# Turning similarities and one-hots on VectorE in 32 by 32 blocks instead of on TensorE, with a reordered first head pair

## The chip, the cores and the metric

One core of a Trainium2 chip. A core has a matrix engine (TensorE, PE in the profile; its weight loads are listed apart as PEld), a vector engine (VectorE, DVE), a scalar engine (ScalarE, ACT), a general engine (GpSimd, POOL) and DMA queues, which run beside each other and wait for each other by semaphores. Matrix products land in PSUM; the other data is in SBUF, both with 128 partitions. The metric is the device time of one execution in microseconds (us), the median of several.

## What is computed

Routing attention, followed by a mixture of experts. Each query and each key of a head goes to the nearest of 16 centroids, and a query sees only the keys with the same centroid. The result is the input of eight experts, of which each row uses one.

```python
# q, k, v: (4, 8, 768, 64) f32; centroids: (8, 16, 64)
q_assign = np.argmax(np.einsum('bhsd,hcd->bhsc', q_n, c_n), axis=-1)   # q_n, k_n, c_n: normalised
k_assign = np.argmax(np.einsum('bhsd,hcd->bhsc', k_n, c_n), axis=-1)
mask = q_assign[:, :, :, None] == k_assign[:, :, None, :]
scores = scale * np.matmul(q, k.transpose(0, 1, 3, 2))                 # scale = 1/8
scores = np.where(mask, scores, -1000000000.0)
attn = softmax(scores)                                                 # written out in the reference
x = np.matmul(attn, v)                                                 # -> (3072, 512) rows
# experts: logits = x @ w_gate; e = argmax; y = relu(x @ w1[e]) @ w2[e], times the gate
```

## The kernel before

The kernel handles two heads at a time, a "pair"; there are 16 pairs g = 0..15, four to a batch. The 768 queries of a pair are taken in two halves of 384 (HS), and the keys in six blocks of 128: 12 score units a pair, six (NB) to a "turn" of the schedule, so two turns a pair. P = 128, S = 768, NQ = 6, D = 64, C = 16, G = 24.

For each pair, rows of q and k are transposed by PE into `qk` (64 numbers of two heads on 128 partitions, tokens along the columns). PE then takes the similarities with the centroids; a second set of transposes brings the tokens back onto the partitions; the largest one is found along the columns and made a one-hot; and a third set of transposes puts the one-hots back, centroids on partitions, where they enter the score products as extra rows that make a score hugely negative if the centroids differ.

```python
def turn(g, piece):                       # transposes of q and k rows, copies to qk
    ...
    n = 4 if piece else 8
    for i in range(n):
        w, j = divmod(8 * piece + i, NQ)
        nc.tensor.transpose(ps[:, i * P : (i + 1) * P], rows[g, "qk"[w]][:, j]..., ident)
    if piece == 0:
        if g == 1: nc.scalar.mul(flat[:, 0:S], ps[:, 0:S], D**-0.5)
        else:      nc.vector.tensor_scalar_mul(flat[:, 0:S], ps[:, 0:S], D**-0.5)
        nc.scalar.copy(flat[:, S:1024], ps[:, S:1024])
    else:
        nc.scalar.copy(flat[:, 1024 : 2 * S], ps[:, 0 : 2 * S - 1024])

def similar(g):                           # 4 products into four groups of 32 partitions
    ...
    nc.vector.tensor_copy(sims[g], ps[:, 0:HS])

def similar2(g):                          # tokens onto partitions
    ...
    for i in range(NQ // 2):
        nc.tensor.transpose(ps[:, i * P : (i + 1) * P], simT[:, i * P : (i + 1) * P], ident)
    nc.scalar.copy(sims[g], ps[:, 0:HS]...)

def assign(g):
    nc.vector.tensor_reduce(mx, sim, axis=AX, op=ALU.max)
    nc.vector.tensor_tensor(sim, sim, mx..., op=ALU.is_ge)
    nc.gpsimd.tensor_tensor(sim, sim, first_c..., op=ALU.mult)    # the first of equals

def assign2(g):
    nc.vector.tensor_reduce(top, rank, axis=AX, op=ALU.max)
    for w in range(2):
        nc.vector.tensor_tensor(ohs..., rank..., top..., op=ALU.is_equal)

def put(g):                               # centroids onto partitions again
    ps = wide()[:, 0, :].bitcast(BF16)
    for j in range(NQ):
        nc.tensor.transpose(ps[:, j * P : (j + 1) * P], ohs..., ident_b)
    nc.scalar.copy(oh[:, 0, :], ps[:, 0:S])
    for a in range(2):
        nc.vector.tensor_scalar(oh[a * D : a * D + C, 1, :], ps[...], scalar1=BIG, scalar2=-BIG, op0=ALU.mult, op1=ALU.add)

def score(u):                             # one unit: 2 products with qk, 2 with ohT, then exp
    ps = ps_s.tile([P, 2, 512], F32, name="sps")
    ...                                   # lhsT=qk[g][r, 1, ks], rhs=qk[g][r, 0, qs]
    ...                                   # lhsT=ohT[g][r, 1, ks], rhs=ohT[g][r, 0, qs]
    nc.scalar.activation(A[u], ps[:, :, 0:HS], AF.Exp)
    ...                                   # DVE: T += A[u], the row sums
```

`wide()` takes one of three PSUM buffers named `sps`, in rotation. Every engine works its instructions off in program order. In each turn n the order is: the six scores, the jobs of part 0, the six products with v (`attend`), the jobs of part 1:

```python
at(n - 3, 0, turn, g, 0); at(n - 3, 0, turn, g, 1)      # n = 2 g, for g of 2 and more
at(n - 3, 1, similar, g)
at(n - 2, 0, similar2, g)
at(n - 2, 0, assign, g); at(n - 2, 0, assign2, g)
at(n - 1, 0, put, g)
at(n, 1, finish, g, 0); at(n + 1, 1, finish, g, 1)
at(n + 2, 0, weigh, g); at(n + 2, 1, weigh2, g)         # logits of the experts
at(n + 2, 1, x_turn, g, 0); at(n + 3, 1, x_turn, g, 1)
# at the end of a batch: at(n + 3, 0, gate, ...), at(n + 3, 1, keep_rows, ...)
```

So in odd turns part 0 holds `put` of the next pair and `turn` of the one after it.

Of the kernel before, what the change touches and what calls it, by code (L numbers as in the profile page):

```python
# [185 lines left out]
def kernel(  # L186
# [77 lines left out]
    ps_m = late.enter_context(tc.tile_pool(name="ps_m", bufs=1, space=PSUM))  # L264

    pools = dict(s=ps_s)


    def wide():
        return pools["s"].tile([P, 2, 512], F32, name="sps")  # L270
# [394 lines left out]
    with ExitStack() as actx:  # L665
# [17 lines left out]
        def load_qk(g):  # L683
            b, hp = divmod(g, HP)
            for name, src in (("q", q), ("k", k)):
                t = rows[g, name] = ld.tile([P, NQ, 2, D], F32, name=name + "_in")
                for a in range(2):
                    nc.sync.dma_start(out=t[:, :, a, :], in_=src[b, 2 * hp + a].rearrange("(p j) d -> p j d", j=NQ))

        def load_v(g):  # L690
            b, hp = divmod(g, HP)
# [5 lines left out]

        csb = consts.tile([P, D], F32)
        nc.scalar.dma_start(out=csb, in_=centroids.rearrange("h c d -> (h c) d"))
        wg_in = consts.tile([P, DB, E], F32)  # L700
        nc.scalar.dma_start(out=wg_in, in_=moe_w_gate.rearrange("(a p) e -> p a e", p=P))
        for f in (load_qk, load_v):
            for g in range(2):
                f(g)
        make_identity(nc, ident)
        nc.vector.tensor_copy(ident_b, ident)

        ps = ps_m.tile([P, 512], F32, name="mps")
        for i in range(12):
            nc.tensor.matmul(ps[:, 0:P], lhsT=ident, rhs=ident, start=True, stop=True)  # L710
        first_c = iota("first_c", [P, C], [[-1, C]], C, 0)
        first_e = iota("first_e", [P, E], [[-1, E]], E, 0)

# [2 lines left out]
        one_row = consts.tile([P, 32], F32)  # L716
        nc.gpsimd.memset(one_row, 0.0)
        nc.gpsimd.memset(one_row[:, E : E + 1], 1.0)
        for a in range(2):
            r = slice(a * D, (a + 1) * D)  # L720
            nc.gpsimd.tensor_copy(wg[r, :, a, 0:E], wg_in[r])

        ohs = ohp.tile([P, NQ, 2, 2, 32], BF16, name="oh")
        nc.gpsimd.memset(ohs, 0.0)
        ohTs = []
        for i in range(2):
            t = ohp.tile([P, 2, S], BF16, name=f"ohT{i}")
            nc.gpsimd.memset(t[:, 1, :], 0.0)
            ohTs.append(t)


        csq = consts.tile([P, D], F32)
        cs2 = consts.tile([P, 1], F32)
        nc.scalar.activation(csq, csb, AF.Square, accum_out=cs2)
        cnrm = consts.tile([P, 1], F32)
        nc.scalar.activation(cnrm, cs2, AF.Sqrt)

# [9 lines left out]
        cn = consts.tile([P, 2, D], F32)  # L747
        for a in range(2):
            nc.vector.tensor_scalar(cn[:, a, :], csb, scalar1=cinv[:, 0:1], scalar2=None, op0=ALU.mult)
        cps = ps_m.tile([P, 512], F32, name="mps")  # L750
        nc.tensor.transpose(cps[:, 0:P], cn.rearrange("p a d -> p (a d)"), ident)

        cblk = consts.tile([P, HP, 2, C], F32)
        nc.gpsimd.memset(cblk, 0.0)
        cview = cps[:, 0:P].rearrange("p (g a c) -> p g a c", a=2, c=C)
        for a in range(2):
            nc.vector.tensor_copy(cblk[a * D : (a + 1) * D, :, a, :], cview[a * D : (a + 1) * D, :, a, :])


        qk, sims, ohT = {}, {}, {}  # L760
# [1 line left out]
        def turn(g, piece):  # L762

            if piece == 0:
                qk[g] = qkp.tile([P, 2, S], F32, name="qk")
            ps = ps_s.tile([P, 2, 512], F32, name="sps").rearrange("p a c -> p (a c)")
            n = 4 if piece else 8
            for i in range(n):
                w, j = divmod(8 * piece + i, NQ)
                nc.tensor.transpose(ps[:, i * P : (i + 1) * P], rows[g, "qk"[w]][:, j].rearrange("p a d -> p (a d)"), ident)  # L770
            flat = qk[g].rearrange("p w s -> p (w s)")
            if piece == 0:

                if g == 1:
                    nc.scalar.mul(flat[:, 0:S], ps[:, 0:S], D**-0.5)
                else:
                    nc.vector.tensor_scalar_mul(flat[:, 0:S], ps[:, 0:S], D**-0.5)
                nc.scalar.copy(flat[:, S:1024], ps[:, S:1024])
            else:
                nc.scalar.copy(flat[:, 1024 : 2 * S], ps[:, 0 : 2 * S - 1024])  # L780

        def similar(g):

            ps = wide()[:, 0, :]
            for t in range(4):
                w, half = divmod(t, 2)
                nc.tensor.matmul(  # L787
                    ps[t * 2 * C : (t + 1) * 2 * C, 0:HS], lhsT=cblk[:, g % HP].rearrange("p a c -> p (a c)"),
                    rhs=qk[g][:, w, half * HS : (half + 1) * HS], start=True, stop=True,
                )  # L790
            sims[g] = asg.tile([P, HS], F32, name="simT", bufs=1)
            nc.vector.tensor_copy(sims[g], ps[:, 0:HS])

        def similar2(g):
            simT = sims.pop(g)
            ps = wide()[:, 0, :]
            for i in range(NQ // 2):
                nc.tensor.transpose(ps[:, i * P : (i + 1) * P], simT[:, i * P : (i + 1) * P], ident)
            sims[g] = asg.tile([P, G, C], F32, name="sim")
            nc.scalar.copy(sims[g], ps[:, 0:HS].rearrange("p (t c) -> p t c", c=C))  # L800

        def assign(g):

            sim = sims.pop(g)
            mx = asg.tile([P, G], F32, name="mx")
            nc.vector.tensor_reduce(mx, sim, axis=AX, op=ALU.max)
            nc.vector.tensor_tensor(sim, sim, mx.unsqueeze(2).to_broadcast([P, G, C]), op=ALU.is_ge)  # L807
            nc.gpsimd.tensor_tensor(sim, sim, first_c[:, None, :].to_broadcast([P, G, C]), op=ALU.mult)  # L808
            sims[g] = sim

        def assign2(g):
            rank = sims.pop(g)
            top = asg.tile([P, G], F32, name="top")
            nc.vector.tensor_reduce(top, rank, axis=AX, op=ALU.max)

            v = lambda t, w: t.rearrange("p (i w x) c -> p i w x c", w=2, x=4)[:, :, w]
            for w in range(2):
                nc.vector.tensor_tensor(
                    ohs.rearrange("p (i h) a w c -> p i (h a) w c", h=2)[:, :, :, w, 0:C], v(rank, w),
                    top.rearrange("p (i w x) -> p i w x", w=2, x=4)[:, :, w].unsqueeze(3).to_broadcast([P, NQ // 2, 4, C]),  # L820
                    op=ALU.is_equal,
                )

        def put(g):
            oh = ohT[g] = ohTs[g % 2]
            ps = wide()[:, 0, :].bitcast(BF16)
            for j in range(NQ):
                nc.tensor.transpose(
                    ps[:, j * P : (j + 1) * P],
                    ohs[:, (j % (NQ // 2)) * 2 + j // (NQ // 2)].rearrange("p a w c -> p (a w c)"), ident_b,  # L830
                )

            nc.scalar.copy(oh[:, 0, :], ps[:, 0:S])
            for a in range(2):
                nc.vector.tensor_scalar(
                    oh[a * D : a * D + C, 1, :], ps[a * D + 32 : a * D + 32 + C, 0:S],
                    scalar1=BIG, scalar2=-BIG, op0=ALU.mult, op1=ALU.add,
                )


        A, T, O = {}, {}, {}
# [6 lines left out]
        def score(u):  # L848
# [8 lines left out]
                r = slice(a * D, (a + 1) * D)  # L857
                nc.tensor.matmul(ps[:, a, 0:HS], lhsT=ohT[g][r, 1, ks], rhs=ohT[g][r, 0, qs], start=False, stop=True)  # L858
            A[u] = ap.tile([P, 2, HS], F32, name="A")
            nc.scalar.activation(A[u], ps[:, :, 0:HS], AF.Exp)  # L860
            if j == 1:
                T[g, half] = tp_.tile([P, 2, HS], F32, name="T", bufs=3)
                nc.vector.scalar_tensor_tensor(  # L863
# [109 lines left out]
        def at(n, part, f, *a):  # L973
            jobs.setdefault((n, part), []).append((f, a))
# [7 lines left out]
        for g in range(NG):  # L982
            n = g * TG
            if g == 0:
                at(-4, 0, turn, g, 0)
                at(-4, 1, turn, g, 1)
                at(-3, 0, similar, g)
                at(-3, 1, similar2, g)
            elif g == 1:

                at(-2, 1, turn, g, 0)
                at(-2, 1, turn, g, 1)
                at(-1, 1, similar, g)
                at(0, 0, similar2, g)
            else:
                at(n - 3, 0, turn, g, 0)
                at(n - 3, 0, turn, g, 1)
                at(n - 3, 1, similar, g)
                at(n - 2, 0, similar2, g)
            at(n - 2, 0, assign, g)  # L1000
            at(n - 2, 0, assign2, g)
            at(n - 1, 0, put, g)
            at(n, 1, finish, g, 0)
            at(n + 1, 1, finish, g, 1)
            if g < NG - 1:
                at(n + 2, 0, weigh, g)
# [313 lines left out]
```

## Time and profile before

| | |
|---|---|
| time, median of 3 | 777.03 us (776.28 to 777.63) |
| span of the profiled execution | 776.7 us |
| the attention part | until about 400 us; the experts after it |
| L787, similarities (DVE copy L792 after it) | 128 products of 384 columns; copies 0.56 us |
| L798, transposes of the similarities | 48 of 128x128 f32 |
| L828, transposes of the one-hots | 96 of 128x128 bf16 |
| L867 and L863, row sums on DVE | 0.96 us each, five a turn |
| L835, DVE part of `put` | 0.55 us each, two a pair |

The page of the profile has the busy time of each engine over the span, then the span in 40 slices with the busy tenths of each. The order of time lists the start and length of each group of instructions, the engine, the line of the kernel, and what is written from what; in square brackets it gives the idle time of the engine ahead of it and what ended that. A table by stretches gives, for each stretch of time, the busy time of each engine with its instructions in parentheses, and the clock granted to PE as a share of its full speed.

### The profile page before, as it was taken

What the parts mean: (1) busy time and instruction counts of PE and PEld (TensorE: products, weight loads), DVE (VectorE), ACT (ScalarE), POOL (GpSimd) and SP (SyncE); (2) the same over time, 40 slices, a digit from 0 to 9 for tenths busy, and PEclk for the clock granted to TensorE, in tenths of its full rate; (3) what the DMA queues carried; (4) which work ended last, traced back from release to release, by engine and by line L of the source; (5) the groups of instructions that cost most, each with busy time, mean ns of one, the idle gap of its engine ahead of it and who ended that gap; (6) DMA issues with size and microseconds to landing.
All of it is one profiled execution on the core that took longest, in us unless ns stands there. A gap on an engine that the chain in (4) does not pass through costs nothing.

```text
span 776.7 us, 12417 instructions
## 1 busy us (share of the span) xinstructions
PE 755.2 (97%) x5021; PEld 485.7 (63%) x5021; DVE 449.8 (58%) x758; ACT 299.0 (38%) x481; POOL 111.0 (14%) x157
## 2 busy tenths in 40 slices
PE   6999999999999999999999999999999999999994
PEld 4544555445554455544556668787888898787861
DVE  3667677666676666778743544555564655555200
ACT  4545645556455564555531112232222214132210
POOL 2200000100000000001200541311312121211101
PEclk9999999999999999999999999999999999999998
DMA  9025501455115221120103446747556675847540
GB/s 221 6 62 204 136 26 37 144 208 131 30 33 144 62 62 31 32 103 1 45 1 135 152 127 224 267 166 253 221 216 219 246 261 178 308 155 246 212 156 18
DMA packets 85281, 106.41 MB, mean 137 GB/s; under 512 B 52831, under 2 KB 56927, under 8 KB 84704
## 3 DMA queue, kind: packets, MB, share of 16 engines
q1 hardware_dynamic: 79616, 85.99, 34.9%
q0 software_dynamic: 4928, 19.51, 6.8%
q8 instruction: 41, 0.67, 0.4%
q14 instruction: 24, 0.20, 0.1%
q10 hardware_dynamic: 672, 0.05, 0.1%
HBM read 92.90 MB, written 13.16 MB: 137 GB/s over the span
## 4 chain that ended last, share of the span: by engine, by line
PE 80%; issue 9%; DVE 6%; POOL 2%; ACT 2%; ACTq 0%; POOLq 0%; DVEq 0%
PE sps L855 15%; PE O L875 13%; PE sps L476 10%; PE sps L310 9%; PE sps L498 8%; PE sps L364 7%; PE sps L858 4%; PE mps L896 3%; DVE T L867 3%; PE sps L787 2%; PE sps L344 2%; PE sps L770 2%; PE sps L291 2%; PE sps L941 1%; PE mps L909 1%
## 5 line engine op out<-in xcount | busy, mean ns | idle before, releaser
L860 ACT ACTIVATE A<-sps 128x768 f32<-128x768 f32 x192 | 153.3, 812 | 53.4 <-PE sps L858 52.3
L855 PE MATMUL sps<-qk 64*128 64x384 f32 x768 | 160.6, 497 | 0.1
L867 DVE TENSOR_TENSOR T<-T,A 128x768 f32<-128x768 f32 x128 | 122.7, 959 | 14.4 <-ACT lsT L902 0.5
L875 PE MATMUL O<-A,v_in 128*64 128x384 f32 x768 | 130.9, 490 | 0.0
L855 PEld LDWEIGHTS sps<-qk 64*128 64x128 f32 x768 | 66.9, 189 | 50.4 <-issue 42.3
L875 PEld LDWEIGHTS O<-A,v_in 128*64 128x64 f32 x768 | 52.2, 137 | 62.6 <-issue 62.5
L858 PE MATMUL sps<-ohT 64*128 64x384 bf16 x384 | 63.6, 325 | 0.0
L364 PE MATMUL sps<-w,h_sb 128*128 128x512 f32 x144 | 63.1, 592 | 0.0
L310 PEld LDWEIGHTS sps<-xgT,w 128*128 128x128 f32 x512 | 58.3, 192 | 4.5 <-issue 2.5
L863 DVE SCALAR_TENSOR_TENSOR T<-A 128x768 f32<-128x768 f32 x32 | 30.7, 958 | 49.1 <-ACT A L860 49.1
L310 PE MATMUL sps<-xgT,w 128*128 128x128 f32 x512 | 58.7, 275 | 0.0
L328 POOL DMA_INDIRECT out_dram<-zo,s_idx x32 | 33.3, 1041 | 154.2 <-ACT zo L324 90.9
L274 POOL DMA_INDIRECT xg<-x_rows,g_idx x32 | 37.7, 1179 | 112.8 <-ACT gate L284 100.9
L808 POOL TENSOR_TENSOR sim<-sim,first_c 128x384 f32<-128x384 f32 x16 | 16.0, 999 | 264.2 <-DVE sim L807 264.2
L364 PEld LDWEIGHTS sps<-w,h_sb 128*128 128x128 f32 x144 | 26.7, 190 | 30.6 <-issue 30.6
L883 ACT COPY xT<-O 128x384 f32<-128x384 f32 x32 | 15.5, 483 | 62.1 <-PE O L875 62.0
L476 PEld LDWEIGHTS sps<-xs,w1s 128*128 128x128 f32 x288 | 36.0, 190 | 4.2 <-DVE xs L387 4.2
L476 PE MATMUL sps<-xs,w1s 128*128 128x144 f32 x288 | 37.8, 288 | 0.0
L324 ACT ACTIVATE zo<-sps,gate 128x512 f32<-128x512 f32 x12 | 8.2, 687 | 72.1 <-PE sps L364 60.1
L858 PEld LDWEIGHTS <-ohT 64*128 64x128 bf16 x384 | 19.5, 95 | 25.3 <-issue 0.6
L297 DVE COPY xgT<-sps 128x512 f32<-128x512 f32 (+1 forms) x20 | 10.8, 566 | 40.6 <-PE sps L291 40.6
L498 PE MATMUL sps<-w2s,hs 128*128 128x256 f32 x144 | 33.6, 383 | 0.0
(246 smaller groups left out, 988.2 us busy)
## 6 DMA issues: line engine op xcount, KB each, us to landing
w<-in_moe_w_dram SPq DMA_DIRECT2D x32, 2048.0 KB, 9.2
x_rows<-x POOLq DMA_DIRECT2D x4, 1548.0 KB, 6.5
q_in<-in_q_dram SPq DMA_DIRECT2D x32, 192.0 KB, 4.4
k_in<-in_k_dram SPq DMA_DIRECT2D x32, 192.0 KB, 4.8
v_in<-in_v_dram SPq DMA_DIRECT2D x16, 384.0 KB, 3.3
xg<-x_rows,g_idx POOLq DMA_INDIRECT x32, 4.5
out_dram<-zo,s_idx POOLq DMA_INDIRECT x32, 5.5
csb<-in_centroids_dram ACTq DMA_DIRECT2D x1, 32.0 KB, 1.9
```

The costliest lines, as they stand in the source:

```text
L274: nc.gpsimd.indirect_dma_start(out=g["xg"][0:m, j, :], out_offset=None, in_=x_d[0 : g["rows"], :], in_offset=bass.IndirectOffsetOnAxis(ap= ...
L310: nc.tensor.matmul(o, lhsT=g["w"][0][:, c, fb * P : (fb + 1) * P], rhs=g["xT"][:, c, :cols], start=(c == 0), stop=(c == DB - 1),)
L328: ins = nc.gpsimd.indirect_dma_start(out=out[:, :], out_offset=bass.IndirectOffsetOnAxis(ap=g["si"](j)[0:m], axis=0), in_=zo[0:m], in_offs ...
L364: nc.tensor.matmul(zp, lhsT=g["h"][:, fb, j * P : (j + 1) * P], rhs=g["w"][1][:, fb, :], start=(fb == 0), stop=(fb == FB - 1),)
L476: nc.tensor.matmul(o, lhsT=a[:, c, f * P : (f + 1) * P], rhs=b[:, c, :], start=(c == 0), stop=(c == KH - 1),)
L498: nc.tensor.matmul(ps[:, 0, 0:DH], lhsT=a[:, f, :], rhs=b[:, f, :], start=(f == 0), stop=(f == FH - 1),)
L855: nc.tensor.matmul(ps[:, a, 0:HS], lhsT=qk[g][r, 1, ks], rhs=qk[g][r, 0, qs], start=True, stop=False)
L858: nc.tensor.matmul(ps[:, a, 0:HS], lhsT=ohT[g][r, 1, ks], rhs=ohT[g][r, 0, qs], start=False, stop=True)
L860: nc.scalar.activation(A[u], ps[:, :, 0:HS], AF.Exp)
L863: nc.vector.scalar_tensor_tensor(T[g, half], in0=A[u - 1], scalar=1e-9 / P, in1=A[u], op0=ALU.add, op1=ALU.add)
L867: nc.vector.tensor_tensor(T[g, half], T[g, half], A[u], op=ALU.add)
L875: nc.tensor.matmul(O[g, half][a * D : (a + 1) * D, 0:HS], lhsT=rows[g, "v"][:, a, j, :], rhs=a_[:, a, :], start=(j == 0), stop=(j == NQ - 1),)
```

## The change

DVE can transpose within blocks of 32 by 32. The layout is arranged so that this is enough: similarities of one 32-row group of partitions (two heads with 16 centroids) are turned in place, the one-hot is found, and the same block turn puts it back. The transposes by PE, the PSUM buffers for them and two copies by ACT go. Since the block turn leaves each group on its own partitions, eight small DVE operations carry the one-hots to where the score products want them; a per-partition scalar (`big`) takes over the choice of the head.

```diff
 def turn(g, piece):
-    n = 4 if piece else 8
+    n = NQ - 4 if piece else 4                # q and k of the same columns in one piece
...
-            nc.vector.tensor_scalar_mul(flat[:, 0:S], ps[:, 0:S], D**-0.5)
-        nc.scalar.copy(flat[:, S:1024], ps[:, S:1024])
+        apart(                                # no order between the two
+            nc.vector.tensor_copy(qk[g][:, 0, 0:512], ps[:, 0:512]),
+            nc.scalar.copy(qk[g][:, 1, 0:512], ps[:, 512:1024]),
+        )
 def similar(g):
-    nc.vector.tensor_copy(sims[g], ps[:, 0:HS])
+    nc.vector.transpose(sims[g], ps[:, 0:HS])
-def similar2(g): ...
 def assign2(g):
-    for w in range(2): ...                    # two comparisons
+    nc.vector.tensor_tensor(groups_of(oh), rank, top..., op=ALU.is_equal)
+    nc.vector.transpose(sims[g], oh)          # bf16, 128x384
 def put(g):
-    ...                                       # six transposes, a copy by ACT, two operations by DVE
+    for half in range(2):
+        for a in range(2):
+            nc.vector.tensor_copy(oh[r, 0, cols], t[q])                     # 32x384 bf16
+            nc.vector.tensor_scalar(oh[r, 1, cols], t[k], scalar1=big[k, a, 0:1], scalar2=big[k, a, 1:2], ...)
 def score(u):
-    nc.scalar.activation(A[u], ps[:, :, 0:HS], AF.Exp)
+    nc.scalar.activation(A[u], ps[:, :, 0:HS], AF.Exp, scale=D**-0.5)
 # the schedule, g of 2 and more
-    at(n - 2, 0, similar2, g)
-at(n - 2, 0, assign, g)
-at(n - 2, 0, assign2, g)
-at(n - 1, 0, put, g)
+    at(n - 2, 0, assign, g)
+    at(n - 1, 0, assign2, g)
+    at(n - 1, 0, put, g)
```

For the first two pairs there is more. The first pair's k is loaded by ACT's queue beside q on the queue of SyncE; the gate weights are loaded later; the first pair's assignment is done by DVE without GpSimd and directly after its similarities; the second pair's assignment comes later; the transposed centroids are made between the two pieces of the first turn; and 18 products whose result nobody reads ("idle") are put after the second pair's transposes, where PE waits for the first one-hots.

```diff
-nc.sync.dma_start(out=t[:, :, a, :], in_=src[...])
+(nc.scalar if g == 0 and name == "k" else nc.sync).dma_start(out=t[:, :, a, :], in_=src[...])
...
 at(-4, 0, turn, g, 0)                         # g == 0
+at(-4, 0, blocks)
 at(-4, 1, turn, g, 1)
 at(-3, 0, similar, g)
-at(-3, 1, similar2, g)
+at(-3, 0, assign, g); at(-3, 0, assign2, g); at(-3, 0, put, g)
...
 at(-2, 1, turn, g, 0); at(-2, 1, turn, g, 1)  # g == 1
-at(-1, 1, similar, g); at(0, 0, similar2, g)
+at(-2, 1, idle_of, 18)
+at(0, 0, similar, g); at(0, 1, assign, g)
+at(1, 0, assign2, g); at(1, 0, put, g)
```

More of the change, by code (lines that the diff above doesn't have):

```diff
@@ L266, with apart @@
     pools = dict(s=ps_s)
+    def apart(first, second):
+        first, second = (getattr(i, "ins", i) for i in (first, second))
+        tc.declare_no_dep(second, first, reason="other banks and other elements")
     def wide():
@@ L687, in load_qk @@
                 for a in range(2):
-                    nc.sync.dma_start(out=t[:, :, a, :], in_=src[b, 2 * hp + a].rearrange("(p j) d -> p j d", j=NQ))
+                    (nc.scalar if g == 0 and name == "k" else nc.sync).dma_start(
+                        out=t[:, :, a, :], in_=src[b, 2 * hp + a].rearrange("(p j) d -> p j d", j=NQ)
+                    )
         def load_v(g):
@@ L699 @@
         nc.scalar.dma_start(out=csb, in_=centroids.rearrange("h c d -> (h c) d"))
-        wg_in = consts.tile([P, DB, E], F32)
-        nc.scalar.dma_start(out=wg_in, in_=moe_w_gate.rearrange("(a p) e -> p a e", p=P))
         for f in (load_qk, load_v):
@@ L704, with idle, idle_of @@
                 f(g)
+        wg_in = consts.tile([P, DB, E], F32)
+        nc.scalar.dma_start(out=wg_in, in_=moe_w_gate.rearrange("(a p) e -> p a e", p=P))
         make_identity(nc, ident)
         nc.vector.tensor_copy(ident_b, ident)
+        def idle(ps, n):
+            for i in range(n):
+                nc.tensor.matmul(ps[:, 0:P], lhsT=ident, rhs=ident, start=True, stop=True)
+        def idle_of(n):
+            idle(ps_m.tile([P, 512], F32, name="mps"), n)
         ps = ps_m.tile([P, 512], F32, name="mps")
-        for i in range(12):
-            nc.tensor.matmul(ps[:, 0:P], lhsT=ident, rhs=ident, start=True, stop=True)
+        idle(ps, 13)
+        cblk = consts.tile([P, HP, 2, C], F32)
+        nc.gpsimd.memset(cblk, 0.0)
         first_c = iota("first_c", [P, C], [[-1, C]], C, 0)
@@ L718 @@
         nc.gpsimd.memset(one_row[:, E : E + 1], 1.0)
+        ohTs = []
+        for i in range(2):
+            t = ohp.tile([P, 2, S], BF16, name=f"ohT{i}")
+            nc.gpsimd.memset(t, 0.0)
+            ohTs.append(t)
+        part_i = consts.tile([P, 1], I32)
+        nc.gpsimd.iota(part_i, pattern=[[0, 1]], base=0, channel_multiplier=1)
+        nc.vector.tensor_scalar(
+            part_i, part_i, scalar1=4, scalar2=1, op0=ALU.arith_shift_right, op1=ALU.bitwise_and
+        )
+        big = consts.tile([P, 2, 2], F32)
+        nc.vector.tensor_copy(big[:, 1, 0:1], part_i)
+        nc.vector.tensor_scalar_mul(big[:, 1, 0:1], big[:, 1, 0:1], BIG)
+        nc.vector.tensor_scalar(big[:, 0, 0:1], big[:, 1, 0:1], scalar1=-1.0, scalar2=BIG, op0=ALU.mult, op1=ALU.add)
+        for a in range(2):
+            nc.vector.tensor_scalar_mul(big[:, a, 1:2], big[:, a, 0:1], -1.0)
         for a in range(2):
@@ L721 @@
             nc.gpsimd.tensor_copy(wg[r, :, a, 0:E], wg_in[r])
[L723 to L729, printed above, removed]
         csq = consts.tile([P, D], F32)
         cs2 = consts.tile([P, 1], F32)
-        nc.scalar.activation(csq, csb, AF.Square, accum_out=cs2)
+        nc.vector.tensor_tensor(csq, csb, csb, op=ALU.mult)
+        nc.vector.reduce_sum(cs2, csq, axis=AX)
         cnrm = consts.tile([P, 1], F32)
@@ L749, with blocks @@
             nc.vector.tensor_scalar(cn[:, a, :], csb, scalar1=cinv[:, 0:1], scalar2=None, op0=ALU.mult)
[L750 to L757, printed above, removed]
+        def blocks():
+            cps = ps_m.tile([P, 512], F32, name="mps")
+            nc.tensor.transpose(cps[:, 0:P], cn.rearrange("p a d -> p (a d)"), ident)
+            cview = cps[:, 0:P].rearrange("p (g a c) -> p g a c", a=2, c=C)
+            for a in range(2):
+                nc.vector.tensor_copy(cblk[a * D : (a + 1) * D, :, a, :], cview[a * D : (a + 1) * D, :, a, :])
         qk, sims, ohT = {}, {}, {}
@@ L765, in turn @@
                 qk[g] = qkp.tile([P, 2, S], F32, name="qk")
-            ps = ps_s.tile([P, 2, 512], F32, name="sps").rearrange("p a c -> p (a c)")
-            n = 4 if piece else 8
[L768 to L771, printed above, removed]
-            if piece == 0:
[L774 to L778, printed above, removed]
+            n = NQ - 4 if piece else 4
+            ps = wide().rearrange("p a c -> p (a c)")
+            for i in range(2 * n):
+                w, j = divmod(i, n)
+                nc.tensor.transpose(
+                    ps[:, i * P : (i + 1) * P], rows[g, "qk"[w]][:, 4 * piece + j].rearrange("p a d -> p (a d)"), ident
+                )
+            if piece == 0:
+                apart(
+                    nc.vector.tensor_copy(qk[g][:, 0, 0:512], ps[:, 0:512]),
+                    nc.scalar.copy(qk[g][:, 1, 0:512], ps[:, 512:1024]),
+                )
             else:
-                nc.scalar.copy(flat[:, 1024 : 2 * S], ps[:, 0 : 2 * S - 1024])
+                nc.scalar.copy(qk[g][:, :, 512:S], ps[:, 0 : 2 * n * P].rearrange("p (w s) -> p w s", w=2))
         def similar(g):
@@ L790, in similar, with groups_of @@
                 )
-            sims[g] = asg.tile([P, HS], F32, name="simT", bufs=1)
-            nc.vector.tensor_copy(sims[g], ps[:, 0:HS])
[L794 to L800, printed above, removed]
+            sims[g] = asg.tile([P, HS], F32, name="sim")
+            nc.vector.transpose(sims[g], ps[:, 0:HS])
+        def groups_of(t):
+            return t.rearrange("p (t c) -> p t c", c=C)
         def assign(g):
-            sim = sims.pop(g)
+            sim = groups_of(sims[g])
             mx = asg.tile([P, G], F32, name="mx")
@@ L807, in assign @@
             nc.vector.tensor_tensor(sim, sim, mx.unsqueeze(2).to_broadcast([P, G, C]), op=ALU.is_ge)
-            nc.gpsimd.tensor_tensor(sim, sim, first_c[:, None, :].to_broadcast([P, G, C]), op=ALU.mult)
-            sims[g] = sim
+            (nc.gpsimd if g else nc.vector).tensor_tensor(
+                sim, sim, first_c[:, None, :].to_broadcast([P, G, C]), op=ALU.mult
+            )
         def assign2(g):
-            rank = sims.pop(g)
+            rank = groups_of(sims.pop(g))
             top = asg.tile([P, G], F32, name="top")
@@ L814, in assign2 @@
             nc.vector.tensor_reduce(top, rank, axis=AX, op=ALU.max)
[L816 to L822, printed above, removed]
@@ L824, in put @@
-        def put(g):
[L825 to L838, printed above, removed]
+            oh = asg.tile([P, HS], BF16, name="oh")
@@ new lines, in assign2 @@
+            nc.vector.tensor_tensor(
+                groups_of(oh), rank, top.unsqueeze(2).to_broadcast([P, G, C]), op=ALU.is_equal
+            )
+            sims[g] = asg.tile([P, HS], BF16, name="ohs")
+            nc.vector.transpose(sims[g], oh)
+        def put(g):
+            t, oh = sims.pop(g), ohTs[g % 2]
+            ohT[g] = oh
+            for half in range(2):
+                cols = slice(half * HS, (half + 1) * HS)
+                for a in range(2):
+                    r = slice(a * D, a * D + 32)
+                    q = slice(half * 32, half * 32 + 32)
+                    k = slice(D + half * 32, D + half * 32 + 32)
+                    nc.vector.tensor_copy(oh[r, 0, cols], t[q])
+                    nc.vector.tensor_scalar(
+                        oh[r, 1, cols], t[k], scalar1=big[k, a, 0:1], scalar2=big[k, a, 1:2], op0=ALU.mult, op1=ALU.add
+                    )
@@ L985 @@
                 at(-4, 0, turn, g, 0)
+                at(-4, 0, blocks)
                 at(-4, 1, turn, g, 1)
                 at(-3, 0, similar, g)
-                at(-3, 1, similar2, g)
+                at(-3, 0, assign, g)
+                at(-3, 0, assign2, g)
+                at(-3, 0, put, g)
             elif g == 1:
@@ L992 @@
                 at(-2, 1, turn, g, 1)
-                at(-1, 1, similar, g)
-                at(0, 0, similar2, g)
+                at(-2, 1, idle_of, 18)
+                at(0, 0, similar, g)
+                at(0, 1, assign, g)
+                at(1, 0, assign2, g)
+                at(1, 0, put, g)
             else:
```

## The prediction

> **What bounds the kernel now.** I read the page first. Its busy lines and the slices say that TensorE (PE) sets the time, with VectorE (DVE) second:
>
> ```profile
> PE 755.2 (97%) x5021; PEld 485.7 (63%) x5021; DVE 449.8 (58%) x758; ACT 299.0 (38%) x481; POOL 111.0 (14%) x157
> ...
> PE   6999999999999999999999999999999999999994
> ...
> DVE  3667677666676666778743544555564655555200
> ```
>
> A digit is a slice of 19.4 us. The change touches only the attention part (slices 1 to 21, up to about 400 us). There PE is full but DVE is at 6 to 8 tenths, so moving work from PE to DVE looks free. Whether it is depends on where in the loop DVE has its room, so next I read the order of time. One head pair takes two turns of six score units. Its length, read from one pair to the next at the maximum of L814, is 23.9 us (198.0 to 221.9). Pairs in which a batch ends take 25.3 us (221.9 to 247.2). This is PE in the odd turn of a common pair (start, length, line):
>
> ```profile
> 204.60 0.51 PE L828 MATMUL sps<-ident_b,oh 128*128 128x128 bf16 x6
> 204.95 0.83 PE L770 MATMUL sps<-ident,q_in 128*128 128x128 f32 x6
> 205.61 0.82 PE L770 MATMUL sps<-ident,k_in 128*128 128x128 f32 x6
> 206.36 4.09 PE L875 MATMUL O<-A,v_in 128*64 128x384 f32 x24
> 210.38 0.55 PE L941 MATMUL sps<-ident,xT 128*128 128x128 f32 x3
> 210.86 0.85 PE L787 MATMUL sps<-qk,cblk 128*32 128x384 f32 x8
> ```
>
> No gaps: one-hots turned, next pair's q and k turned, attend, x turned, similarities, and at 211.64 the next scores. By start to start the six one-hot transposes hold PE for 0.35 us, not their summed 0.51. The three similarity transposes hold it for 0.48 us (218.11 to 218.59, in the even turn). Now DVE in the same odd turn:
>
> ```profile
> 203.38 4.15 DVE L867 TENSOR_TENSOR T<-T,A 128x768 f32<-128x768 f32 x4
> 207.55 1.12 DVE L835 TENSOR_SCALAR ohT<-sps 16x768 bf16<-16x768 bf16 x2
> 208.71 0.96 DVE L777 TENSOR_SCALAR qk<-sps 128x768 f32<-128x768 f32 x1
> 210.96 0.56 DVE L944 TENSOR_TENSOR x<-sps,rd 128x384 f32<-128x384 f32 x1 [1.30 <-PE sps L941]
> ```
>
> The row sums T end only at 207.53, because they follow the exponentials. Then come L835 (part of the one-hots) and L777 (the turned q); ACT's L778 may only follow L777 and ends at 210.07. PE wants the result at 210.86. So DVE's room here is under 0.8 us, though over the pair it is idle for some 7 us (19.98 busy of the 28 us from 203 to 231). The pair with a gate shows what happens when more is put into that stretch:
>
> ```profile
> 227.60 4.14 DVE L867 TENSOR_TENSOR T<-T,A 128x768 f32<-128x768 f32 x4 [0.46 <-DVE T L863]
> 231.67 0.20 DVE L953 TENSOR_REDUCE lmax<-lg 128x6 f32<-128x48 f32 x1
> ...
> 233.10 1.12 DVE L835 TENSOR_SCALAR ohT<-sps 16x768 bf16<-16x768 bf16 x2
> 234.25 0.96 DVE L777 TENSOR_SCALAR qk<-sps 128x768 f32<-128x768 f32 x1
> ...
> 235.67 1.33 PE L787 MATMUL sps<-qk,cblk 128*32 128x384 f32 x8 [0.78 <-ACT qk L778]
> ...
> 236.93 0.92 PE L855 MATMUL sps<-qk 64*128 64x384 f32 x4
> ```
>
> Small gate operations push L835 back by 1.45 us (231.65 to 233.10). PE then waits at L787, and this pair is 1.4 us longer than the others. A delay of DVE here is passed on to PE almost whole.
>
> Last the beginning:
>
> ```profile
> 14.00:16.00 2.00, 0.00 (x0) 0.00 (x0) 1.10 (x3) 0.53 (x2) 0.83 (x1) 0.94 1.25 242
> 16.00:18.00 2.00, 1.87 (x14) 0.76 (x14) 0.26 (x2) 0.80 (x1) 0.00 (x0) 0.50 1.25 275
> 18.00:20.00 2.00, 2.00 (x10) 0.90 (x8) 1.49 (x3) 0.00 (x0) 0.00 (x0) 0.50 1.25 197
> 20.00:22.00 2.00, 2.00 (x10) 1.22 (x10) 0.00 (x0) 0.88 (x2) 0.00 (x0) 0.50 0.05 11
> ```
>
> The columns are PE, PEld, DVE, ACT, POOL busy, then the granted clock. PE is idle at 14 to 16 us, waiting for the first one-hots, and then runs at a clock of 0.50 until about 22.7. The first score group ends at 25.5.
>
> [...]
>
> **The change, part by part.**
> *PE, every pair:* minus 0.48 (similarity transposes) minus 0.35 (one-hot transposes) = -0.83 us, were nothing else to happen; over 15 pairs 12.5 us. ACT loses two copies (0.48 and 0.79); it has room, and this saves nothing by itself.
>
> *DVE, odd turn:* the built order puts the rest of the assignment and all of `put` between the row sums and the copy of the next q. Working:
> - L814-like maximum 0.55 and comparison 0.56 (384 columns at the length of L807), with 0.03 between: 1.17;
> - the bf16 block turn: [...] with its gap 0.60;
> - eight operations of 32x384 bf16. [...] 0.25 to 0.27[...]: 2.1. [...]
> - the q copy, now 512 columns from PSUM, 0.69 as L297.
>
> Together 4.6 us after the row sums. Counted from the start of the turn's scores (199.55), the row sums end at 8.0, so the copy ends at 12.6 and, with 0.1 to the PE start (9.07 to 9.21 at the first pair), similarities start at 12.7. PE, at L787 after 11.31 before (210.86), would be ready at 11.31 - 0.35 = 10.96. So PE waits 1.75 us. The next scores start at 12.7 + 0.8 = 13.5, against 12.09 before: +1.4. The even turn gives back 0.48. Net +0.95 us a pair.
> The block turn of the similarities replaces a copy (0.56 to about 0.58) ahead of row sums that today wait 2.13 us: free. Dropping the scaling of q into the exponential costs nothing.
>
> *Pairs concerned:* odd turns 3 to 27, thirteen of them, times 0.95 = +12.4. In turn 29 no q is left to turn, but the next scores wait for `put`: some +0.8 more. Gate pairs should behave alike, since their old delay stays.
>
> *Beginning:* the loads of the first q and k go out on two queues at about 0.8 to 2 us and, at 4.4 to 4.8 us from issue to landing (part 6 of the page), are there by about 6.3; before, the first turns start at 7.0. Then 0.9 for the first eight transposes, about 1.5 for the rest and the copies (0.69 on DVE, 0.59 twice on ACT), 0.85 for the similarities at full clock: they end near 9.6. From there all is DVE: block turn 0.6, maximum, comparison, rank, maximum, comparison at 0.58 each, block turn 0.6, `put` 2.1, 6.2 in sum: one-hots at about 16, against 18.96 before (17.82 + 1.14). The idle products should keep the clock up, so that the rest of the first score group runs in about 4.4 us (a whole group of six takes 5.0 at full clock, 199.55 to 204.6) instead of 5.75 (19.76 to 25.5). One-hots 3 us earlier plus 1.35 us of clock plus the 0.48 of this pair's similarity transposes: about 5.2 us gained by turn 2.
>
> *Sum:* 777.0 - 5.2 + 12.4 + 0.8 = 785.0 us.
>
> **Rivals.**
> 1. *PE bound alone:* DVE's added work is hidden, as its busy share (58%) suggests. Then -12.5 - 5 = 759.5 us. Against it speaks the gate pair: 1.45 us of DVE delay cost 1.4. For it, that PE's slack of 0.35 to 0.8 absorbs part, and short operations might overlap.
> 2. *The eight small operations are slower* ([...] a dear scalar operand read per partition). Each 0.1 us on each is 0.8 us a pair, 11 us in all[...]. For it: the trace before has no bf16 copy from one group of partitions to another, and its only scalar operation with an operand per partition (L749, 523 and 658 ns for 64 columns) is long, though GpSimd was filling buffers beside it.
> 3. *Only the beginning counts:* `put` costs 1.2 us, the waits just eat the PE gain, and 772 remains.
>
> **Range and chances.** The middle is 785. The duration of `put`, 1.3 to 3.2 us, moves it from 773 to 800; the beginning is uncertain by 3 us. Range 767 to 801. Faster by over 2% (below 761.5) needs rival 1 nearly whole: 0.07. Slower by over 2% (above 792.6) needs small operations of about 0.35: 0.23. Within 2%: 0.70.
>
> **What would show it.** In the profile after: no L798 or L828 kinds on PE; an idle stretch of PE ahead of the similarities, released by the DVE copy of q, of 1 to 2.5 us in every odd turn; pairs of about 24.8 us instead of 23.9; the small one-hot operations near 0.26 us; the first score group ending near 20 at full clock. The prediction is wrong if PE shows no such wait (then the time is near 760), or if DVE's row sums themselves fall behind from turn to turn.

## The result, and the profile after

The changed kernel takes 816.2 us (median of 4, 814.96 to 817.61) against 777.33 us: a ratio of 1.050, with a 95% interval of 1.048 to 1.052. It is slower by 38.9 us, where the prediction had 8 us and a range that ended at 801. The head of the page of the changed kernel:

```profile
PE 763.8 (94%) x4915; PEld 487.2 (60%) x4915; DVE 477.0 (59%) x864; ACT 282.1 (35%) x445; POOL 110.5 (14%) x156
...
PE   8898889888988898889899999999999999999995
...
DVE  5756676667666765777784453655555556555200
...
PEclk9999999999998999999999999999999999999998
```

PE has 106 instructions fewer, yet is busy longer (763.8 against 755.2 us) and at the same time has holes in the attention part that it did not have before. DVE's share is 59%, against 58% before: by that number alone it has room. A pair now takes 26.9 us (197.4 to 224.4 at the maximum, now L838) instead of 23.9.

The order of time of the changed kernel in an odd turn shows the hole (start, length, engine, line):

```profile
197.45 0.54 DVE L838 TENSOR_REDUCE top<-sim 128x24 f32<-128x384 f32 x1
198.03 0.56 DVE L840 TENSOR_TENSOR oh<-sim,top 128x384 bf16<-128x384 f32 x1
198.62 0.58 DVE L845 STREAM_TRANSPOSE ohs<-oh 128x384 bf16<-128x384 bf16 x1
199.23 0.25 DVE L856 COPY ohT<-ohs 32x384 bf16<-32x384 bf16 x1
199.49 0.37 DVE L857 TENSOR_SCALAR ohT<-ohs,big 32x384 bf16<-32x384 bf16 x1
...
201.86 0.69 DVE L802 COPY qk<-sps 128x512 f32<-128x512 f32 x1
...
202.69 0.85 PE L813 MATMUL sps<-qk,cblk 128*32 128x384 f32 x8 [2.07 <-DVE qk L802]
203.48 1.11 PE L876 MATMUL sps<-qk 64*128 64x384 f32 x4
...
204.69 1.50 PE L876 MATMUL sps<-qk 64*128 64x384 f32 x4
...
216.47 0.92 PE L876 MATMUL sps<-qk 64*128 64x384 f32 x4
...
230.39 0.92 PE L876 MATMUL sps<-qk 64*128 64x384 f32 x4
...
231.31 0.81 PE L876 MATMUL sps<-qk 64*128 64x384 f32 x4
```

PE stands still for 2.07 us ahead of the similarities until DVE has copied q. The first five lines are the start of what stands before that copy. So far this is the predicted picture. What the prediction did not have is in the L876 lines: at 204.69 four score products take 1.50 us instead of 0.81 (at 231.31, one of the places where they ran at full speed). The turn that starts at 203.48 lasts until 216.47, 12.99 us. The table by stretches for a similar place (PE, PEld, DVE, ACT, POOL busy, then the granted clock, the busy share of the DMA engines and GB/s) says why:

```profile
64.00:66.00 2.00, 0.88 (x7) 0.31 (x3) 1.91 (x7) 0.48 (x1) 0.00 (x0) 1.00 0.20 20
66.00:68.00 2.00, 1.05 (x10) 0.32 (x10) 1.35 (x4) 0.00 (x0) 0.00 (x0) 0.88 1.01 377
68.00:70.00 2.00, 2.00 (x8) 1.19 (x10) 0.56 (x1) 0.12 (x1) 0.00 (x0) 0.50 1.02 387
70.00:72.00 2.00, 2.00 (x14) 0.89 (x12) 0.00 (x0) 1.39 (x2) 0.00 (x0) 0.76 1.00 401
```

After the wait the clock is at 0.50 for 3.41 us (67.54 to 70.95). PE counts as fully busy there while its products take nearly twice as long (1.50 against 0.81 us for the four above), which is why its busy time rose.

Two readings of the waits of the whole run and of the group of L857 complete the picture (the first: waiter, releaser, total us, times, longest; the second: total us and mean ns):

```profile
PE sps L813 <- DVE qk L802: 34.5, 14, 3.4
```

```profile
L857 DVE TENSOR_SCALAR ohT<-ohs,big 32x384 bf16<-32x384 bf16 x64 | 23.9, 373 | 1.0
```

### The profile page after: what moved, and what is told of

Read it like the earlier page. It is cut to its first block, busy times and chain, and to the rows that moved or that the text cites. A ratio compares the mean times of both kernels' runs of the same rounds, so it can differ in the third digit from the quotient of the medians.

```text
span 814.8 us, 12258 instructions
## 1 busy us (share of the span) xinstructions
PE 763.8 (94%) x4915; PEld 487.2 (60%) x4915; DVE 477.0 (59%) x864; ACT 282.1 (35%) x445; POOL 110.5 (14%) x156
## 4 chain that ended last, share of the span: by engine, by line
PE 70%; DVE 16%; issue 9%; ACT 2%; POOL 1%; DMA 1%; ACTq 0%; POOLq 0%; DVEq 0%
PE sps L876 16%; PE sps L481 9%; PE O L896 8%; PE sps L315 8%; PE sps L503 8%; PE sps L369 7%; DVE T L888 5%; PE sps L879 4%; DVE ohT L857 3%; PE mps L917 3%; PE sps L813 2%; DVE ohT L856 2%; PE sps L349 2%; ACT A L881 2%; PE sps L296 1%
## 5 line engine op out<-in xcount | busy, mean ns | idle before, releaser
L876 PE MATMUL sps<-qk 64*128 64x384 f32 x768 | 175.8, 538 | 1.3 <-DVE x L965 0.8
L876 PEld LDWEIGHTS sps<-qk 64*128 64x128 f32 x768 | 73.0, 205 | 58.7 <-issue 47.0
L879 PE MATMUL sps<-ohT 64*128 64x384 bf16 x384 | 67.4, 343 | 0.3 <-DVE ohT L857 0.3
L904 ACT COPY xT<-O 128x384 f32<-128x384 f32 x32 | 15.4, 480 | 104.2 <-PE O L896 104.2
L813 PE MATMUL sps<-qk,cblk 128*32 128x384 f32 x128 | 16.5, 574 | 34.7 <-DVE qk L802 34.5
```

Of the source, the lines that this page charges most:

```text
L813: nc.tensor.matmul(ps[t * 2 * C : (t + 1) * 2 * C, 0:HS], lhsT=cblk[:, g % HP].rearrange("p a c -> p (a c)"), rhs=qk[g][:, w, half * HS : ...
L876: nc.tensor.matmul(ps[:, a, 0:HS], lhsT=qk[g][r, 1, ks], rhs=qk[g][r, 0, qs], start=True, stop=False)
```

## The experiments

Three theories stood against each other. A: the DVE operations that now stand between the row sums and the copy of q hold PE, and a PE that stands still also loses its clock. B: DVE has too much work over the whole pair. C: the clock falls for another reason than the wait. All ratios below are against the kernel before, timed on the same chip.

**PE kept busy through the wait.** Eight spare products stand ahead of the similarities. Edit of the changed kernel:

```diff
 def similar(g):
+    if g >= 2:
+        idle_of(8)                 # products whose result nobody reads
```

> The changed kernel with eight idle products ahead of the similarities from the third pair on, where PE waits for the DVE copy of q. Theory A (the wait itself, and a clock that halves because PE stands still): the wait's end stays where it was, PE is busy through it, the clock stays at 1.00 after it, and the half-clock time goes: some 18 us less, 796 to 800. Theory B (DVE has too much work over the whole pair): nothing is gained, 816. Theory C (the clock falls for another reason than the wait): 816 and the same 0.50 stretches.

Measured: 795.6 us, ratio 1.024 (1.022 to 1.026); the mean clock of the run is 0.997 instead of 0.969. The stretches of a pair:

```profile
202.00:228.00 26.00, 25.72 (x189) 13.57 (x187) 18.61 (x33) 12.10 (x17) 1.38 (x3) 1.00 0.19 47
```

20.6 us are gone though PE does more. The length of a turn shows where they went:

```profile
193.41 0.92 PE L878 MATMUL sps<-qk 64*128 64x384 f32 x4
...
204.71 0.92 PE L878 MATMUL sps<-qk 64*128 64x384 f32 x4
...
218.64 0.92 PE L878 MATMUL sps<-qk 64*128 64x384 f32 x4
```

The odd turn, with the hole, is as long as in the changed kernel (13.9 us). Only the even one after it is shorter: 11.30 us, against 12.99. That fits A and rules out C: the half clock comes from the standing still, and it is worth over half of the loss. The full DMA queues of the table above (share 1.00 to 1.02 from 66 to 72) are not its cause either: here they are as full (1.03 from 66 to 70), at a clock of 1.00. DVE's work is what it was.

**Four copies on ACT.** Edit of the changed kernel:

```diff
-nc.vector.tensor_copy(oh[r, 0, cols], t[q])
+(nc.scalar.copy if g else nc.vector.tensor_copy)(oh[r, 0, cols], t[q])
```

> The changed kernel with the four plain copies of the one-hots done by ACT instead of DVE (from the second pair on). Theory A: the DVE stretch ahead of the q copy is about 1.0 us shorter, so the wait falls from 2.1 to about 1.1 us a pair, and the clock dips become rarer or vanish: between 800 (waits alone) and 783 (clock too). Theory B: DVE's work falls by 1.0 of 18.9 us a pair, at most 1 us a pair, 800.

Measured: 794.6 us, ratio 1.025 (1.022 to 1.028), inside the range of A, and B is not excluded by it. The four copies took 0.51 us each on ACT, against 0.25 on DVE, so now ACT came last: PE waited 22.6 us in 13 pairs for ACT's copies of the turned k, which stood behind them, instead of 34.5 for DVE. The clock stayed at 1.00 after the nine waits of 1.34 us and fell after two of the four longer ones (2.6 to 2.7 us).

**The same operations a turn earlier.** Edit of the changed kernel:

```diff
 at(n - 2, 0, assign, g)
-at(n - 1, 0, assign2, g)
-at(n - 1, 0, put, g)
+at(n - 2, 0, assign2, g)
+at(n - 2, 1, put, g)
```

> The changed kernel with the same DVE operations, but the second half of the assignment and the eight small operations one turn (about 12 us) earlier, after the even turn's other work; nothing is taken away. Theory A: the odd turn has only the q copy between row sums and similarities, PE no longer waits, the clock stays up, and the PE work saved shows: 760 to 766, below the kernel before. Theory B: the same total of DVE work, so about 816, or waits of the same sum at another place.

Measured: 775.0 us, ratio 0.997 (0.996 to 0.998). No work was taken from DVE and 41 us are gone, so B falls. But it is 9 us above the range of A. The order of time of this run shows what was missed:

```profile
197.04 0.58 DVE L845 STREAM_TRANSPOSE ohs<-oh 128x384 bf16<-128x384 bf16 x1
197.54 0.23 DVE L933 COPY ls<-mps 128x108 f32<-128x108 f32 x1
...
198.73 0.55 DVE L965 TENSOR_TENSOR x<-sps,rd 128x384 f32<-128x384 f32 x1
...
199.33 0.92 PE L876 MATMUL sps<-qk 64*128 64x384 f32 x4 [0.50 <-DVE x L965]
```

DVE had waited for GpSimd's part of the assignment (16.8 us in 14 waits), and the block turn now delays the work with the logits (L933) and the x copy (L965). The x copy gives a PSUM buffer back, which a score unit needs. The six scores took 5.8 us instead of 5.0 (196.95 to 202.76). The pair is back at 23.85 us: the saved 0.83 us went into this wait.

**A delay put into the kernel before.** Five spare additions of 384 columns on DVE, no block turns:

```diff
 at(n - 1, 0, put, g)
+if 2 <= g < NG - 1:
+    at(n - 1, 0, delay, 5)         # and 2 in the second run
```

> The kernel before with five spare DVE additions of 384 columns (about 3.0 us) ahead of the q copy in the odd turns of pairs 2 to 14; no block turns, all PE transposes kept. Theory A: less 0.3 to 0.7 of room, a PE wait of about 2.4 us in 13 pairs and a clock of half for some 3 us after each (1.6 us lost): about +4.0 x 13 = +52, 825 to 832. Theory B (total DVE load): DVE is at 17 + 3 of 24 us, still below full: 777. Theory C (the dips come from something in the changed kernel other than the wait): waits alone, about +31, 808, at full clock.

> The kernel before with two spare DVE additions (about 1.2 us) instead of five ahead of the q copy in the odd turns of pairs 2 to 14. Theory A: less 0.3 to 0.7 of room, a wait of 0.5 to 0.9 us in 13 pairs, too short to bring the clock down: +7 to +12, 784 to 789. If any wait brings the half clock: +25 and more.

Measured: 826.7 us with five (ratio 1.063, 1.060 to 1.066) and 789.1 us with two (1.016, 1.014 to 1.017). Waits of the run with five, and two stretches of it and one of the run with two:

```profile
PE sps L787 <- ACT qk L778: 33.8, 13, 3.5
```

```profile
122.00:149.00 27.00, 24.41 (x174) 12.14 (x174) 19.36 (x35) 13.20 (x20) 1.20 (x2) 1.00 0.19 45
149.00:175.00 26.00, 23.14 (x153) 11.66 (x155) 16.06 (x26) 12.71 (x19) 2.05 (x4) 0.87 0.35 107
```

```profile
196.00:221.00 25.00, 24.63 (x178) 12.26 (x176) 17.94 (x29) 13.18 (x21) 1.20 (x2) 1.00 0.20 48
```

1.2 us of DVE work cost 11.9/13 = 0.9 us a pair, at full clock: 0.3 us of it went into the room there was. 2.9 us of it cost 49.6/13 = 3.8: a wait of 33.8/13 = 2.6, which is again the delay less 0.3, and for the rest mostly the clock. Nothing of the change is in these kernels, so the loss needs no property of block turns.

**Constants in place of the operand per partition.** Edit of the changed kernel; it leaves out the choice of the head:

```diff
-scalar1=big[k, a, 0:1], scalar2=big[k, a, 1:2]
+scalar1=BIG, scalar2=-BIG
```

> The changed kernel with constants in place of the operand read per partition in the four scalar operations of each pair. This leaves out the choice of the head, so keys of the other head's centroid count too; the time is what is asked. If the per-partition operand is what makes them 0.373 us instead of 0.25: they fall to 0.25, the wait by 0.5 us a pair, and the time by at least 7 us, to 795 to 809, more where a clock dip goes with it. If the operation itself costs 0.373: 816, unchanged.

The time, 6688 us, says nothing: with these one-hots the row sums leave the range that the kernel expects, and its general path runs everything a second time (from 786 us on). The trace of the attention part is usable:

```profile
L857 DVE TENSOR_SCALAR ohT<-ohs x64: 248/251/255, 15.6 to 397.7; 32x384 bf16<-32x384 bf16 x64
```

Lowest, median, highest are 248, 251 and 255 ns: so the two operands per partition cost 0.12 us on each operation, and the waits at L813 fell from 34.5 to 27.5 us, 0.5 a pair, as expected. The gain is larger than that. After the nine waits of a common pair, now 1.57 us instead of 2.07, the clock stayed at 1.00, and the last turn of the attention part starts 22.7 us earlier than in the changed kernel (410.11 against 432.81): 7 us of waits, the rest mostly clock.

**The q copy first.** In the changed kernel the turn of the next q and k is put ahead of the other jobs of part 0:

```diff
-at(n - 3, 0, turn, g, 0)
-at(n - 3, 0, turn, g, 1)
+jobs.setdefault((n - 3, 0), [])[0:0] = [(turn, (g, 0)), (turn, (g, 1))]
```

> The changed kernel with one swap of order on DVE: in the odd turns the q copy comes first behind the row sums, and the rest of the assignment and the eight small operations after it; nothing else moves, no DVE work is taken away. Theory A: the similarities no longer wait; instead the x copy now stands behind the small operations and gives its PSUM buffer back late, which holds the second score unit for about 1.0 us a pair, at full clock. Pairs of about 24.0 us, 776 to 782. Theory B (total DVE work): 816.

Measured: 785.3 us, ratio 1.010 (1.008 to 1.012). The similarities no longer wait, a common pair is 24.0 us (197.46 to 221.50), and PE waits at L876 for the x copy instead, both as expected. The total is 3 us above the range: I had not allowed for the gate operations, which in their pairs lengthen that wait from 0.7 to 1.6 us and bring the clock down again (stretches at 0.93), nor for the first work on the experts, which lengthens it to 2.9 us in turn 28.

**The beginning by itself.** In two kernels on the basis of the one before. The first loads k on ACT's queue and the gate weights later, and has ten idle products; the second has the idle products alone:

```diff
 at(-2, 1, turn, g, 0); at(-2, 1, turn, g, 1)   # g == 1
+at(-2, 1, idle_of, 10)
```

> The kernel before with only part of the new beginning: the first pair's k loaded on ACT's queue, the gate weights later, and ten idle products after the second pair's transposes (all PE transposes of similarities and one-hots kept). If the beginning is worth what the prediction said, mostly by the clock: the 0.50 stretch from 16 to 22 us goes, the first score group ends some 2 us earlier, and the time falls by 2 to 3 us, to 774 to 775. If the beginning is worth nothing behind the DVE chain of the second pair: 777.

> The kernel before with nothing changed but ten idle products after the second pair's transposes, where PE waits for the first one-hots. If the half clock at the start costs what the prediction put on it (1.35 us, with the second pair's similarities some 1.9): 775 to 776. If the chain of row sums in the second turn ends last anyway: 777, no difference.

Measured: 781.8 us (ratio 1.006, 1.005 to 1.007) and 776.3 us (0.9990, 0.9981 to 0.9998). The first is a miss, and my edit is its cause rather than the change: it took the loads and left the order of the work beside them. ACT issued k before it squared the centroids (first table load at 3.28 instead of 1.70 us), and GpSimd waited 5.63 us for the late gate weights and filled the centroid blocks only after that, at 10.71; the q copy began at 11.43 instead of 8.10. In the change the square is DVE's and the fill comes first. So this run says nothing on the worth of the two queues. The second keeps the clock at 1.00 from 12 to 64 us, where it had been at 0.50 from 16 to 22, and gains 1.0 us.

**The operations spread over DVE's gaps.** On the changed kernel, and in a second step the later constants too:

```diff
 at(n - 3, 1, similar, g)
-at(n - 2, 0, assign, g)
-at(n - 1, 0, assign2, g)
-at(n - 1, 0, put, g)
+at(n - 3, 1, assign, g)            # where DVE waited for exponentials
+at(n - 2, 0, assign2, g)
+at(n - 2, 0, put, g, (0,))         # first half
+at(n - 2, 1, put, g, (1,))         # second half, behind the x copy
 ...                                # second pair: assign, assign2 and put one part or more earlier
-at(0, 1, place_consts)             # second step
+at(-1, 1, place_consts)
```

> The changed kernel with the same DVE operations placed where DVE is idle: maximum and comparison right behind the block turn of the similarities in the odd turn (DVE waited 2.05 us for exponentials there), the rest of the assignment and half of the small operations behind the even turn's row sums (it waited 1.2 us for GpSimd there), the other half after the x copy. Theory A: no PE wait and no late x copy (which cost the run with everything earlier 0.8 us a pair), so the full 0.83 us a pair shows: 760 to 766. Theory B: no gain over 775.

> The spread version, with one more move: GpSimd builds the later constants before the first scores instead of behind the second pair's rank, so that DVE doesn't wait for them. In the spread version the wait of PE at the third pair's similarities was 4.3 us, and the clock was near 0.57 for 8 us after it. Theory A: that wait falls below 1 us and the dip goes: 4 to 7 us less, 762 to 765.

Measured: 769.1 us (ratio 0.990, 0.988 to 0.991) and 762.8 us (0.982, 0.981 to 0.983). The first missed its range by 3 us through one wait of 4.3 us at the third pair, where DVE waited for constants from GpSimd; the second step took that away. In the first, a pair is 23.1 us, and PE is full (stretches of 23 us):

```profile
92.00:115.00 23.00, 23.00 (x167) 11.36 (x165) 18.17 (x33) 12.10 (x17) 1.20 (x2) 1.00 0.21 51
115.00:138.00 23.00, 23.00 (x167) 11.31 (x165) 19.02 (x38) 12.23 (x18) 1.21 (x3) 1.00 0.22 51
```

The busy line of the second:

```profile
PE 742.1 (98%) x4915; PEld 478.7 (63%) x4915; DVE 480.7 (63%) x864; ACT 282.0 (37%) x445; POOL 111.5 (15%) x156
```

All 864 DVE instructions of the changed kernel are there, 480.7 us of them, and it is 53 us faster than the changed kernel and 14.6 us faster than the one before. B is out. With the same 4915 instructions PE is busy for 742.1 us instead of 763.8: most of the difference is the half clock (mean clock 0.996 against 0.969). Of PE's saving of 0.83 us a pair 0.74 shows once nothing waits (23.13 against 23.87), and the gate pairs' extra 1.4 us are gone too, because their gate operations no longer stand in a full stretch. In the profiled executions about 5 us of the gain stand before turn 3 (it starts at 50.01 instead of 55.05), so they come from the new beginning and the second pair's earlier operations.

## Why the prediction was wrong

The direction and the first part of the mechanism were right: the DVE chain of the odd turn took the place of the PE work removed. The sum was short by 31 us. Two steps failed, and the second cost so much only because of the first. Point by point:

- *DVE order, room and passing on to PE:* right. The wait is at the place named and has the releaser named. The kernel before with a delay shows the same.
- *The block turns:* right. The bf16 one took 0.578 us, where the sum had 0.60 with its gap, a figure that no run had shown before; the f32 one from PSUM took 0.582.
- *The eight small operations, "0.25 to 0.27":* the first step that failed; no run had shown this figure before. Right for the four copies (0.250), wrong for the four scalar operations (0.373). The reason is the operand per partition, as the run with constants shows (0.251). This was in rival 2, at a smaller size. It made the wait 2.07 us instead of 1.57 and a pair 0.5 us longer, 6 us in 13 turns.
- *The net per pair, "+0.95 us":* the second step that failed. As a sum of waits it was good: with constants a common pair took 24.73 us, 0.86 more than before. But it had no term for PE's clock. At the 1.75 us that it foresaw it may have needed none, for in common pairs none of nine waits of 1.34 us (copies on ACT) and none of nine of 1.57 us (constants) was followed by half clock; at 2.07 us seven of nine were, and a pair took 26.9 us instead of 25.2. The prediction read the clock of 0.50 after PE's idle stretch at 14 to 16 us and did not ask what would follow its own waits.
- *"Gate pairs should behave alike":* right. At full clock, with PE kept busy, they take 26.5 us against 25.2; before, 25.3 against 23.9. Their waits of 3.3 us hold the old delay too.
- *The beginning, "about 5.2 us gained by turn 2":* too large. Turn 1 starts at 27.03 instead of 29.96, 2.9 us earlier, and turn 2 only 1.8 (41.44 instead of 43.27; 2.5 with PE kept busy). The first one-hots were ready at 18.0 instead of 16, since PE began at 6.9 and the first copies, behind a table load on ACT and the centroid chain on DVE, only at 8.5. Then the second pair's operations hold PE in turn 1, which the prediction, counting from turn 3, left out; in the second spread version, which has them earlier, turn 2 starts at 38.72. The gain from the clock was estimated at 1.35 us; alone, it gave 1.0.

The trace of the changed kernel shows more of the clock. The 24 changes of the granted clock in its attention part (40.23, 43.64, 67.54, 70.95 and so on) all lie whole multiples of 3.413 us apart, though a pair takes 26.9 us. Two waits of 2.07 us had two outcomes, as these stretches between points whole multiples of 3.413 us from those changes show:

```profile
200.66:204.07 3.41, 1.38 (x12) 0.59 (x14) 2.84 (x7) 0.02 (x1) 0.00 (x0) 1.00 0.78 200
204.07:207.48 3.41, 3.41 (x15) 1.66 (x12) 0.21 (x2) 1.62 (x2) 0.00 (x0) 0.50 0.68 147
...
227.96:231.38 3.42, 1.77 (x16) 0.82 (x18) 2.59 (x6) 0.00 (x0) 0.00 (x0) 1.00 0.92 234
231.38:234.79 3.41, 3.41 (x28) 1.95 (x26) 1.52 (x2) 3.22 (x5) 0.00 (x0) 1.00 0.52 113
```

The wait that ended at 202.69 lay almost whole in one stretch: PE was idle for 2.03 us of it, and the next stretch ran at 0.50. The wait that ended at 229.61 was cut in two at 227.96: 1.65 us of it lay in the stretch behind that point, and the clock stayed at 1.00.

Put together from the starts of turns 3, 29 and 31 in the profiled executions. Before:

```profile
55.05 0.92 PE L855 MATMUL sps<-qk 64*128 64x384 f32 x4
...
371.59 0.92 PE L855 MATMUL sps<-qk 64*128 64x384 f32 x4
...
394.69 0.92 PE L855 MATMUL sps<-qk 64*128 64x384 f32 x4
```

The changed kernel with PE kept busy, then turn 31 alone of the changed kernel and of the one with constants:

```profile
52.10 0.92 PE L878 MATMUL sps<-qk 64*128 64x384 f32 x4
...
387.33 0.92 PE L878 MATMUL sps<-qk 64*128 64x384 f32 x4
...
411.81 0.92 PE L878 MATMUL sps<-qk 64*128 64x384 f32 x4
```

```profile
432.81 0.92 PE L876 MATMUL sps<-qk 64*128 64x384 f32 x4
```

```profile
410.11 0.92 PE L876 MATMUL sps<-qk 64*128 64x384 f32 x4
```

At full clock the change costs 17.1 us by turn 31, against 8.0 predicted: 2.2 us less were gained by turn 3, the thirteen pairs cost 18.7 instead of 12.4 (the operand per partition), and the last turns 1.4 instead of 0.8. The clock adds 21.0, and 38.1 is the whole loss of the profiled executions (spans of 776.7 and 814.8). With constants the loss by turn 31 is 15.4 us, clock included; an estimate from that is some 792 us for the change with small operations as fast as foreseen, inside the range. So 0.12 us on four operations cost not 6 us but 22.7, because they took the wait from a length after which the clock stayed to one after which it mostly fell.

## What to carry to other kernels

DVE's share of busy time (58% before, 59% in the changed kernel, 63% in the fastest) didn't say whether it could take more work: ask in which stretch the new work stands, and what leaves that engine right after it. If PE then waits, the wait need not be all of the cost: here seven of nine waits of 2.07 us were followed by 3.4 us at half clock, and none of nine of 1.57 us was; eight products that nobody reads showed in one run how much of the loss was clock (20.6 of 38.9 us). And before giving up on moved work, move it in time: the same instructions made this kernel 5% slower in one place and, with constants built earlier, 1.8% faster in others.

## What the runs showed of the hardware

- A bf16 scalar operation on 32x384 took 0.251 us with constants and 0.373 with two operands read per partition; a plain copy took 0.250.
- The same copy on ACT took 0.51 us, and on DVE 0.25.
- A 32 by 32 block turn by DVE took little more than a copy of the size: 0.582 us for 128x384 f32 from PSUM, where the copy it replaced took 0.558; 0.578 us for 128x384 bf16.
- An exponential of 128x768 on ACT took 0.812 us on average in the kernel before, without the scale of q, and in the changed kernel, with it.
- In common pairs, PE's clock went to 0.50 after seven of nine waits of 2.07 us, and after none of nine of 1.57 us or of nine of 1.34 us. In the changed kernel's attention part its 24 changes lay whole multiples of 3.413 us apart.
